# Full-size transposes and last-key products in an attention and MLP kernel on one core

## The chip, the core and the metric

The kernel runs on one core of a Trainium2 chip. The core has five engines that run beside each other and wait for each other by semaphores: TensorE (matrix products; the profile calls it PE, its weight loads PEld), VectorE (DVE), ScalarE (ACT), GpSimd (POOL) and SyncE (SP), which issues most of the DMAs. The metric is the time of one execution on the device in microseconds; of several runs the median counts.

A matrix product on TensorE loads one operand into the array (the weights: so many rows of the array, so many columns) and streams the other through it. In the profile "128\*32 128x128" is a product with 128 rows and 32 columns of the array in use, over a moving operand of 128 rows and 128 columns.

## The reference

Four batches pass through three stages: attention with a decay, a mixing stage of two Fourier transforms with an MLP, and a gated MLP.

```python
scores = scale * np.matmul(q, k.transpose(0, 1, 3, 2))      # 4 x 8 heads, 576 tokens, 64 wide
cum = np.cumsum(np.log(np.clip(f, 0.0001, 1.0)), axis=-1)
scores = np.where(causal, -1e9, scores + cum[:, :, :, None] - cum[:, :, None, :])
scores = scores - np.max(scores, axis=-1, keepdims=True)
attn = np.exp(scores)
attn = attn / (np.sum(attn, axis=-1, keepdims=True) + 1e-09)
x = np.matmul(attn, v)                                       # heads side by side: 4 x 576 x 512
...
u = x + np.real(np.fft.fft(np.fft.fft(x, axis=1), axis=2))
un = (u - mu) / np.sqrt(var + 1e-06)
x = u + np.maximum(un @ w_ch1, 0.0) @ w_ch2                  # 512 -> 2048 -> 512
...
h = np.maximum(x @ w_in, 0.0)                                # 512 -> 1024, halves u and v
v_s = np.einsum('ts,bsd->btd', w_spatial, v_n) + b_spatial[None, :, None]
out = (u * v_s) @ w_out
```

## The kernel before

Each float32 operand is split into two float16 parts, high and low, and a product is made of three float16 products. A batch is handled in steps: the four pairs of heads one after the other (attention), then the folded Fourier transforms, the norm, the MLP of the mixing stage (lines 1052 and 1077: `ph` is the first product, `acc` the second) and the gated MLP (`pu`, `pvv`, `vs`, `po`). While the MLPs of one batch run, the attention of the next is woven in between. TensorE executes in the order in which the code issues: a long written list of steps (`START`) for batch 0 and the attention of batch 1, then tables of times. For the last batches the order on the other engines is set by a scheduler from its own estimates.

For a pair of heads the steps are these. `attn_stack` transposes q and k and sends them by DMA into the tiles `S` (S1 and S2 in the code, two of each in turn). `attn_max` makes the scores once, coarsely, and takes the row maxima with DVE into `mcol`, for five tiles of queries (`QSTART`, `QWIDE`: 128, 128, 64, 128 and 128 queries) and two heads. Its last part, `rows`, writes the negated maxima in two float16 parts into columns 30 and 31 of `mc`, a tile of 128 partitions with 32 columns for each head and query tile, zero elsewhere. Ten transposes (line 692, `mxt`) turn these into rows 96 to 127 of a PSUM tile, and ACT (line 697) and DVE (line 699, one column) copy them into `S`. So the second product of the scores (lines 729 and 733, `sc`) subtracts the maximum as it goes. `mcol` and `mc` exist once and serve all pairs.

`attn_scores` turns the scores into exponentials in `P`, keys down the partitions, in four groups. The 576 keys are four tiles of 128 and one of 64; the group with the last 64 has all 128 partitions of `P` written, those beyond the keys as the exponential of a large negative number. `attn_pv` (lines 797 to 799) multiplies with `vh`, the split v with a column of ones behind each head, of which the sum of the exponentials comes out: `P` is loaded into the array, 65 columns of `vh` are streamed. For the last key tile (`kt == 4`) 64 rows of both were used. `v_prep` allocates `vh` and sets the ones on POOL (line 495), and `v_split` fills it.

Of the first pair of batch 2 the program issues no transposes, so there are 15 groups of ten.

Of the kernel before, what the change touches and what calls it, by code (L numbers as in the profile page):

```python
# [13 lines left out]
F16 = mybir.dt.float16  # L14
# [42 lines left out]
QWIDE = [128, 128, 64, 128, 128]  # L57
# [123 lines left out]
def tile_kernel(  # L181
# [25 lines left out]
    V, A, G, T = nc.vector, nc.scalar, nc.gpsimd, nc.tensor  # L207

    cp = ctx.enter_context(tc.tile_pool(name="cp", bufs=1))
# [20 lines left out]
    o = 0  # L230
# [6 lines left out]
    for h in range(2):  # L237
        CT.append(tab[:, h, 0:963].rearrange("p (t s) -> p t s", t=3))
        ST.append(tab[:, h, 963:1926].rearrange("p (t s) -> p t s", t=3))
        o = 1926  # L240
# [8 lines left out]
    eyeh = cp.tile([128, 128], F16, name="eyeh")  # L249
# [33 lines left out]
    GT = cp.tile([128, 2, 4, 128], F16, name="GT")  # L283
    gsc = cp.tile([128, 1], F32, name="gsc")
    mcol = cp.tile([128, 2, 5], F32, name="mcol")
    mc = cp.tile([128, 2, 5, 32], F16, name="mc")
    G.memset(mc, 0.0)


    state = {}  # L290
# [5 lines left out]
    def xps(name):  # L296
        return pools["x"].tile([128, 2, 512], F32, name=name, tag="x")
# [51 lines left out]
    def smc(b, i):  # L349
        c = 8 * (b % 2) + i  # L350
        return sm[:, c:c + 1]
# [140 lines left out]

    def v_prep(b, raw):
        vh = rp.tile([128, 2, 5, H, 65], F16, name=f"vh{b}", tag="r10")
        G.memset(vh[:, 0, :, :, 64:65], 1.0)
        state[b]["vh"] = vh
        yield
        mx = rp.tile([128, 2], F32, name="vmx", tag="vmx")
        V.memset(mx, 0.0)
        V.tensor_reduce(  # L500
            out=mx[:, 0:1], in_=raw[:, 0:4, :], axis=AX.XY, op=ALU.max, apply_absolute_value=True
        )
        V.tensor_reduce(
            out=mx[:64, 1:2], in_=raw[:64, 4, :], axis=AX.X, op=ALU.max, apply_absolute_value=True
        )
        V.tensor_tensor(mx[:, 0:1], mx[:, 0:1], mx[:, 1:2], op=ALU.max)
        yield 1
        yield from pow2_scale(mx[:, 0:1], smc(b, 0), smc(b, 1), VT)
        V.tensor_scalar(
            out=smc(b, 2), in0=smc(b, 0), scalar1=smc(b, 0), scalar2=1e-6, op0=ALU.mult, op1=ALU.mult  # L510
        )
        yield
# [79 lines left out]
    def attn_max(b, hp):  # L592
        s = hp % 2

        def mm(ps, j, c0, t, k0, k1, mask=None):
            pe_mask = mask is not None and b in PEMASK
            T.matmul(
                ps[:, j, c0:c0 + k1 - k0],
                S2[s][0:126, j, QSTART[t]:QSTART[t] + 128],
                S2[s][0:126, j, QN + k0:QN + k1],  # L600
                start=True, stop=not pe_mask,
            )
            if pe_mask:
                c1 = c0 + k1 - k0
                T.matmul(ps[:, j, c1 - mask.shape[1]:c1], eyeb, mask, start=False, stop=True)

        junk = mo = None

        def work():
            nonlocal junk, mo  # L610
            if mo is None:
                junk = rp.tile([128, 128], BF16, name="junk", tag="junk")
                mo = rp.tile([128, 2], F32, name="mo", tag="mo", bufs=2)

        def diag(ps, t, c0, n, mask, first):
            for j in range(2):
                V.tensor_tensor_reduce(
                    out=junk[:, 0:n], in0=ps[:, j, c0:c0 + n], in1=mask, scale=1.0,
                    scalar=-3.0e38 if first else mo[:, j:j + 1],
                    op0=ALU.add, op1=ALU.max, accum_out=mcol[:, j, t:t + 1],  # L620
                )

        def off(ps, c0, n, dst=None):
            V.tensor_reduce(out=mo if dst is None else dst, in_=ps[:, :, c0:c0 + n], axis=AX.X, op=ALU.max)  # L624

        def both(ps, t, c0, n, mask):

            m = mask.shape[1]
            if b in PEMASK:
                off(ps, c0, n, mcol[:, :, t])  # L630
            else:
                if n > m:
                    off(ps, c0, n - m)
                diag(ps, t, c0 + n - m, m, mask, n == m)

        def diags():
            work()
            pd = xps("mxd")
            for j in range(2):
                mm(pd, j, 0, 0, 0, 128, n0)  # L640
                mm(pd, j, 128, 1, 0, 256, n0)
            yield 1
            both(pd, 0, 0, 128, n0)
            both(pd, 1, 128, 256, n0)
            yield 1

        def wide():
            work()
            pa = xps("mxa")
            for j in range(2):  # L650
                mm(pa, j, 0, 4, 0, 448)
            yield 1
            off(pa, 0, 448)
            yield 1

        def ends():
            pb = xps("mxb")
            for j in range(2):
                mm(pb, j, 0, 4, 448, 576, n4)
                mm(pb, j, 128, 2, 0, 320, n2)  # L660
            yield 1
            if b in PEMASK:
                off(pb, 0, 128, mcol[:, :, 4])
                V.tensor_tensor(mcol[:, :, 4], mcol[:, :, 4], mo, op=ALU.max)
            else:
                diag(pb, 4, 0, 128, n4, False)
            both(pb, 2, 128, 320, n2)
            yield 1

        def rest():  # L670
            work()
            p3 = xps("mxc")
            for j in range(2):
                mm(p3, j, 0, 3, 0, 448, n3)
            yield 1
            both(p3, 3, 0, 448, n3)
            yield

        def rows():
            V.tensor_tensor(  # L680
                mc[:, :, :, 30], mcol, neg.unsqueeze(2).broadcast_to([128, 2, 5]), op=ALU.mult
            )
            V.scalar_tensor_tensor(
                out=mc[:, :, :, 31], in0=mcol, scalar=-1.0 / 16384.0, in1=mc[:, :, :, 30],
                op0=ALU.mult, op1=ALU.subtract,
            )
            yield 1
            pm = pools["x"].tile([128, 2, 1024], F16, name="mxt", tag="x")
            for j in range(2):
                for t, o in enumerate(QSTART):  # L690
                    n = QWIDE[t]
                    T.matmul(  # L692
                        pm[96:128, j, o:o + n], mc[:n, j, t, :], eyeh[:n, :n],
                        is_transpose=True, start=True, stop=True,
                    )
            yield 1
            A.activation(out=S2[s][96:128, :, 0:S], in_=pm[96:128, :, 0:S], func=AF.Copy)
            yield
            V.tensor_copy(S2[s][96:128, :, S:S + 1], pm[96:128, :, 288:289])
            yield 1  # L700

        return dict(d=diags(), a=wide(), b=ends(), c=rest(), t=rows())


# [80 lines left out]
    def attn_pv(b, hp, P):  # L785
        vh = state[b]["vh"]
        ps = xps("pv")
        for g in range(4):
            for j in range(2):
                h = 2 * hp + j  # L790
                for t, c0, n, kt in ((t, *x[1:]) for t in range(5) for x in PV[t] if x[0] == g):
                    kk = 64 if kt == 4 else 128
                    o0 = 65 * t
                    hi = P[g][:kk, 0, j, c0:c0 + n]
                    lo = P[g][:kk, 1, j, c0:c0 + n]
                    first, last = (g, t) == (0, 0), g == 3 and (t, kt) == PVLAST
                    T.matmul(ps[:n, j, o0:o0 + 65], hi, vh[:kk, 0, kt, h, :], start=first, stop=False)  # L797
                    T.matmul(ps[:n, j, o0:o0 + 64], hi, vh[:kk, 1, kt, h, 0:64], start=False, stop=False)  # L798
                    T.matmul(ps[:n, j, o0:o0 + 65], lo, vh[:kk, 0, kt, h, :], start=False, stop=last)  # L799
            yield  # L800
        yield 1

        if "X" not in state[b]:
            state[b]["X"] = yp.tile([128, 5, DM], F32, name=f"X{b}", tag="X")
        X = state[b]["X"]
        rc = rp.tile([128, 2, 5], F32, name="rc", tag="rc")
        po = ps[:, :, 0:325].rearrange("p j (t d) -> p j t d", d=65)
        V.tensor_scalar(out=rc, in0=po[:, :, :, 64], scalar1=16.0e-9, scalar2=None, op0=ALU.add)
        V.reciprocal(rc, rc)
        V.tensor_tensor(  # L810
            X[:, :, 2 * D * hp:2 * D * hp + 2 * D].rearrange("p t (j d) -> p j t d", j=2),
            po[:, :, :, 0:64], rc.unsqueeze(3).broadcast_to([128, 2, 5, 64]), op=ALU.mult,
        )
        yield 1
# [466 lines left out]
    def xsteps(b, small=False):  # L1281
# [5 lines left out]
        def vload():  # L1287
            raw[b] = v_load(b)
            yield 1
            yield from v_prep(b, raw[b])  # L1290
# [160 lines left out]
```

## Time and profile before

| | before |
|---|---|
| median of 3 runs | 928.03 us (924.24 to 930.45) |
| the profiled execution | 930.1 us, its span 928.3 us |
| TensorE busy, weight loads busy | 834.6 us, 721.4 us |
| DVE, ACT, POOL busy | 570.9, 383.2, 196.5 us |
| mean granted clock of TensorE | 0.967 |

The span runs from the first to the last instruction in the trace; the execution's own time has a little around it. Busy times of TensorE overlap, since products are pipelined: the distance between two starts says what a product costs in a full queue, its duration how long it is under way. A row of the chain of waits says what the end of the program depended on at that time.

### The profile page before, as it was taken

The page shows a single profiled execution, that of the slowest core. Times are in us where ns is not written, and L with a number is a line of the kernel's source. Part 1 is how long each engine was busy: PE and PEld are TensorE (multiplying, and loading weights), DVE is VectorE, ACT ScalarE, POOL GpSimd, SP SyncE. Part 2 cuts the span into 40 slices and gives each one's busy share as a digit, 9 for nine tenths or more (in the row PEclk, how much of TensorE's full clock was granted, in tenths as well). Part 3 has the DMA queues.
Part 4 walks back from the last instruction along what each step waited for, and adds up shares of the span by engine and source line. Part 5 has one row for each costly group of instructions (what it writes and reads, how often), then busy time and mean ns, then how long its engine had stood idle before and what let it go on. Part 6 is the DMA issues. An engine that isn't in the chain of part 4 may idle for free.

```text
span 928.3 us, 22154 instructions
## 1 busy us (share of the span) xinstructions
PE 834.6 (90%) x9395; PEld 721.4 (78%) x9395; DVE 570.9 (61%) x1311; ACT 383.2 (41%) x653; POOL 196.5 (21%) x307
## 2 busy tenths in 40 slices
PE   2668359999998998999999998999999999999997
PEld 1456248999997686899997775899997787999784
DVE  5676789897646895746747664747656671123341
ACT  2676656765534433433432442533342432111232
POOL 5276764112013320000005330000004340000010
PEclk9988778999998999999999999999999999999999
DMA  9986157664210008230100017221100001000001
GB/s 184 215 244 224 46 161 178 156 146 122 52 32 5 1 8 180 66 65 2 41 1 2 1 27 172 65 44 23 40 2 1 1 1 47 1 1 2 1 2 57
DMA packets 74835, 60.88 MB, mean 66 GB/s; under 512 B 59680, under 2 KB 60080, under 8 KB 74608
## 3 DMA queue, kind: packets, MB, share of 16 engines
q1 hardware_dynamic: 74016, 58.13, 25.4%
q8 instruction: 74, 1.21, 0.6%
q0 software_dynamic: 720, 1.33, 0.5%
q14 instruction: 25, 0.20, 0.1%
HBM read 40.43 MB, written 4.83 MB: 49 GB/s over the span
## 4 chain that ended last, share of the span: by engine, by line
PE 66%; DVE 13%; ACT 9%; DMA 5%; issue 3%; SPq 2%; POOL 1%; ACTq 0%; DVEq 0%; POOLq 0%
PE ph L1052 17%; PE acc L1077 16%; PE vs L1224 5%; PE pu L1158 5%; PE po L1254 4%; PE pvv L1178 3%; DMA S<-a 2%; ACT P L753 2%; PE pv L797 2%; PE pv L799 1%; PE mxt L692 1%; PE sc L729 1%; PE pv L798 1%; PE yps L914 1%; PE sc L733 1%
## 5 line engine op out<-in xcount | busy, mean ns | idle before, releaser
L1052 PE MATMUL ph<-unT,W 128*128 128x192 f16 x2304 | 208.5, 248 | 1.7 <-DVE unT L1019 1.0
L1077 PE MATMUL acc<-hT,W 128*128 128x192 f16 x2304 | 205.1, 246 | 0.0
L1052 PEld LDWEIGHTS <-W 128*128 128x128 f16 x2304 | 193.6, 99 | 6.9 <-issue 2.6
L1077 PEld LDWEIGHTS <-W 128*128 128x128 f16 x2304 | 191.1, 98 | 0.6
L1059 ACT ACTIVATE hT<-ph 128x384 f16<-128x384 f32 x96 | 47.2, 492 | 146.3 <-PE ph L1052 146.1
L1061 DVE SCALAR_TENSOR_TENSOR hT<-ph,hT 128x384 f16<-128x384 f32 x96 | 53.1, 553 | 86.7 <-ACT hT L1059 86.6
L753 ACT ACTIVATE P<-sc,log 128x642 f16<-128x642 f32 (+3 forms) x64 | 59.2, 933 | 63.7 <-DVE sc L746 53.1
L768 DVE TENSOR_TENSOR P<-sc,P 128x1024 f16<-128x1024 f32 (+3 forms) x50 | 49.6, 994 | 38.4 <-ACT sc L766 36.8
L797 PE MATMUL pv<-vh,P 128*128 128x65 f16 (+1 forms) x480 | 59.9, 204 | 3.7 <-DVE mcol L624 2.4
L729 PE MATMUL sc<-S 128*128 128x256 f16 (+2 forms) x288 | 51.9, 242 | 11.0 <-ACT ex L762 4.9
L799 PE MATMUL pv<-vh,P 128*128 128x65 f16 (+1 forms) x480 | 59.0, 201 | 2.0 <-POOL P L764 1.5
L798 PE MATMUL pv<-vh,P 128*128 128x64 f16 (+1 forms) x480 | 59.1, 201 | 0.0
L1224 PE MATMUL vs<-WP,vn 128*128 128x288 f16 x448 | 57.0, 286 | 0.0
L1178 PE MATMUL pvv<-WI,unT 128*128 128x512 f16 (+1 forms) x240 | 55.7, 388 | 0.3 <-ACT vr L1191 0.3
L733 PE MATMUL sc<-S 128*128 128x256 f16 (+2 forms) x288 | 53.1, 242 | 0.0
L1158 PE MATMUL pu<-unT,WI 128*128 128x192 f16 x576 | 52.0, 250 | 0.8 <-ACT gu L1167 0.8
L797 PEld LDWEIGHTS <-P 128*128 128x128 f16 (+1 forms) x480 | 47.8, 104 | 5.5 <-issue 1.8
L1224 PEld LDWEIGHTS <-vn 128*128 128x128 f16 x448 | 43.6, 98 | 10.7
L1158 PEld LDWEIGHTS <-WI 128*128 128x128 f16 x576 | 48.9, 100 | 3.1 <-issue 2.3
L798 PEld LDWEIGHTS <-P 128*128 128x128 f16 (+1 forms) x480 | 48.3, 105 | 2.8 <-issue 2.6
L799 PEld LDWEIGHTS <-P 128*128 128x128 f16 (+1 forms) x480 | 48.4, 105 | 2.6 <-POOL P L764 1.8
L565 POOL COPY a<-a 128x2 f16<-128x2 f16 x32 | 7.1, 229 | 196.4 <-ACT a L557 177.0
(233 smaller groups left out, 1474.6 us busy)
## 6 DMA issues: line engine op xcount, KB each, us to landing
S<-a SPq DMA_DIRECT2D x96, 144.2 KB, 3.9
W<-in_moe_w_ch_dram SPq DMA_DIRECT2D x16, 512.0 KB, 6.6
WI<-in_moe_w_ch_dram SPq DMA_DIRECT2D x16, 512.0 KB, 5.2
a<-in_k_dram SPq DMA_DIRECT2D x32, 144.0 KB, 3.1
a<-in_q_dram SPq DMA_DIRECT2D x32, 144.0 KB, 4.7
vraw<-in_v_dram SPq DMA_DIRECT2D x16, 256.0 KB, 5.1
WP<-in_moe_w_in_dram SPq DMA_DIRECT2D x8, 512.0 KB
out_dram<-ob SPq DMA_DIRECT2D x16, 256.0 KB, 3.0
```

What stands on the lines that cost most here:

```text
L729: T.matmul(ps[:, j, c0:c0 + w], S2[s][:, j, QN + 128 * kt:QN + 128 + 128 * kt], qh, start=i == 0, stop=False,)
L733: T.matmul(ps[:, j, c0:c0 + w], S1[s][:, j, 128 * kt:128 * kt + 128], q1, start=False, stop=last and b not in PEMASK,)
L753: A.activation(out=pt[:, 0], in_=src, func=AF.Exp, scale=1.0 / 2048.0, bias=log16)
L797: T.matmul(ps[:n, j, o0:o0 + 65], hi, vh[:kk, 0, kt, h, :], start=first, stop=False)
L798: T.matmul(ps[:n, j, o0:o0 + 64], hi, vh[:kk, 1, kt, h, 0:64], start=False, stop=False)
L799: T.matmul(ps[:n, j, o0:o0 + 65], lo, vh[:kk, 0, kt, h, :], start=False, stop=last)
L1052: T.matmul(ph[:, c, :], W1[:, a, kc, 128 * ff:128 * ff + 128], unT[:, e, kc, tok(t)], start=(c == 0 and kc == 0 and i == 0), stop=(c == 1 ...
L1061: V.scalar_tensor_tensor(out=hT[:, 1], in0=ph, scalar=0.0, in1=hT[:, 0], op0=ALU.max, op1=ALU.subtract)
L1077: T.matmul(acc[t][d // 2][:, d % 2, :], W2[:, a, ff, 128 * d:128 * d + 128], hT[:, e, c, :], start=(ff == 0 and i == 0 and d % 2 == 0), st ...
L1158: T.matmul(ph[:, c, :], WI[:, a, kc, 128 * ff:128 * ff + 128], xT[:, e, kc, tok], start=(c == 0 and kc == 0 and i == 0), stop=(c == 1 and ...
L1178: T.matmul(pv[:n, :], xT[:, a, kc, 128 * i:128 * i + n], WI[:, e, kc, DM:2 * DM], start=(kc == 0 and j == 0), stop=(kc == 3 and j == 2),)
L1224: T.matmul(ps, vn[:kk, a, s, 128 * c:128 * c + 128], WP[:kk, e, s, tok], start=i == 0, stop=i == len(jobs) - 1,)
```

## The change

The ten transposes of a pair now use all 128 rows and columns: the tile `mc` gets 96 zero columns in front, so that the 128 columns that end with a block can be loaded, and the block still comes out on rows 96 to 127. The 64-wide piece of the third query tile becomes 128 wide; the next piece overwrites what it writes too much. The products over the last 64 keys use 128 rows; for that, the rows 64 to 127 of `vh` in the last key tile are cleared by a memset on POOL before the ones are set.

```diff
-    mc = cp.tile([128, 2, 5, 32], F16, name="mc")
-    G.memset(mc, 0.0)
+    mcw = cp.tile([128, 416], F16, name="mc")
+    mc = mcw[:, 96:].rearrange("p (j t c) -> p j t c", j=2, t=5)
+    G.memset(mcw, 0.0)
...
         vh = rp.tile([128, 2, 5, H, 65], F16, name=f"vh{b}", tag="r10")
+        G.memset(vh[64:128, :, 4], 0.0)
         G.memset(vh[:, 0, :, :, 64:65], 1.0)
...
                 for t, o in enumerate(QSTART):
-                    n = QWIDE[t]
                     T.matmul(
-                        pm[96:128, j, o:o + n], mc[:n, j, t, :], eyeh[:n, :n],
+                        pm[:, j, o:o + 128], mcw[:, 160 * j + 32 * t:160 * j + 32 * t + 128], eyeh,
                         is_transpose=True, start=True, stop=True,
                     )
...
-                    kk = 64 if kt == 4 else 128
                     o0 = 65 * t
-                    hi = P[g][:kk, 0, j, c0:c0 + n]
-                    lo = P[g][:kk, 1, j, c0:c0 + n]
+                    hi = P[g][:, 0, j, c0:c0 + n]
+                    lo = P[g][:, 1, j, c0:c0 + n]
                     first, last = (g, t) == (0, 0), g == 3 and (t, kt) == PVLAST
-                    T.matmul(ps[:n, j, o0:o0 + 65], hi, vh[:kk, 0, kt, h, :], start=first, stop=False)
-                    T.matmul(ps[:n, j, o0:o0 + 64], hi, vh[:kk, 1, kt, h, 0:64], start=False, stop=False)
-                    T.matmul(ps[:n, j, o0:o0 + 65], lo, vh[:kk, 0, kt, h, :], start=False, stop=last)
+                    T.matmul(ps[:n, j, o0:o0 + 65], hi, vh[:, 0, kt, h, :], start=first, stop=False)
+                    T.matmul(ps[:n, j, o0:o0 + 64], hi, vh[:, 1, kt, h, 0:64], start=False, stop=False)
+                    T.matmul(ps[:n, j, o0:o0 + 65], lo, vh[:, 0, kt, h, :], start=False, stop=last)
```

On TensorE no instruction changes its place. On POOL the memset is added in each batch. Between batches 2 and 3, behind the last norms of the batch before (`st`), POOL's order was:

```order
L994 TENSOR_TENSOR st_7684<-st_7684,mhalf 128x1 x3
L994 TENSOR_TENSOR st_7684<-st_7684,mhalf 65x1
L495 MEMSET vh_8168 128x40
L565 COPY a_7447<-a_7447 128x2 x6
L1145 COPY tsc<-sc_8093 128x2
```

The changed kernel has there, with line numbers two or so higher:

```order
L994 TENSOR_TENSOR st_7687<-st_7687,mhalf 128x1 x3
L994 TENSOR_TENSOR st_7687<-st_7687,mhalf 65x1
L496 MEMSET vh_8171 64x2x520
L497 MEMSET vh_8171 128x40
L567 COPY a_7450<-a_7450 128x2 x6
L1145 COPY tsc<-sc_8096 128x2
```

The new memset stands ahead of the old one, and the copies into `a` (the stacks' last columns) behind both. On DVE the scheduler moved one instruction, in the first pair of batch 3, where the scale of v (`sm`) is worked out from its maximum (`p2e`). Before:

```order
L338 TENSOR_SCALAR sm<-p2e 128x1
L342 TENSOR_SCALAR sm<-p2e 128x1
L699 COPY S_0_93<-mxt 32x2
L509 TENSOR_SCALAR sm<-sm 128x1
L522 SCALAR_TENSOR_TENSOR vh_8168<-vraw_8018,sm,vh_8168 128x8x64 x4
```

And now:

```order
L339 TENSOR_SCALAR sm<-p2e 128x1
L343 TENSOR_SCALAR sm<-p2e 128x1
L511 TENSOR_SCALAR sm<-sm 128x1
L700 COPY S_0_93<-mxt 32x2
L524 SCALAR_TENSOR_TENSOR vh_8171<-vraw_8021,sm,vh_8171 128x8x64 x4
```

The copy that completes `S` with the maxima stands one place later, behind the last step of the scale.

## Rows read from the trace of the kernel before

**Rows 1.** The page, TensorE's busy tenths in 40 slices of the span.
```profile
PE   2668359999998998999999998999999999999997
```

**Rows 2.** The page, chain that ended last, by engine and by line.
```profile
PE 66%; DVE 13%; ACT 9%; DMA 5%; issue 3%; SPq 2%; POOL 1%; ACTq 0%; DVEq 0%; POOLq 0%
PE ph L1052 17%; PE acc L1077 16%; PE vs L1224 5%; PE pu L1158 5%; PE po L1254 4%; PE pvv L1178 3%; DMA S<-a 2%; ACT P L753 2%; PE pv L797 2%; PE pv L799 1%; PE mxt L692 1%; PE sc L729 1%; PE pv L798 1%; PE yps L914 1%; PE sc L733 1%
```

**Rows 3.** Line 692: form, count, min/median/max ns, first and last start.
```profile
L692 PE MATMUL mxt<-eyeh,mc x150: 199/219/314, 35.4 to 681.0; 128*32 128x128 f16 x120, 64*32 64x64 f16 x30
```

**Rows 4.** Timeline of TensorE, batch 3: start us, duration us, engine, line.
```profile
678.94 0.19 PE L797 MATMUL pv<-vh,P 128*65 128x65 f16 x1
678.97 0.20 PE L798 MATMUL pv<-vh,P 128*65 128x64 f16 x1
679.01 0.20 PE L799 MATMUL pv<-vh,P 128*65 128x65 f16 x1
679.13 0.22 PE L797 MATMUL pv<-vh,P 64*65 64x65 f16 x1
...
679.35 0.20 PE L797 MATMUL pv<-vh,P 128*128 128x65 f16 x1
679.39 0.19 PE L798 MATMUL pv<-vh,P 128*128 128x64 f16 x1
...
680.02 0.19 PE L799 MATMUL pv<-vh,P 128*128 128x65 f16 x1
680.14 1.09 PE L692 MATMUL mxt<-eyeh,mc 128*32 128x128 f16 x10
681.16 2.15 PE L1052 MATMUL ph<-unT,W 128*128 128x192 f16 x24
```

**Rows 5.** Timeline of TensorE at 78 us, masks with 128 moving columns.
```profile
78.28 0.22 PE L605 MATMUL mxd<-cmt 128*128 128x128 bf16 x1
78.33 0.27 PE L597 MATMUL mxd<-S 126*128 126x256 f16 x1
```

**Rows 6.** Chain in order of time, 545 to 552 us: start us, us, what.
```profile
547.15 0.88 PE tr L1007 x8
548.03 3.44 PE vs L1224 x28
```

**Rows 7.** Groups of instructions by form: busy us, mean ns, idle before.
```profile
L739 PEld LDWEIGHTS <-cmt 128*128 128x128 bf16 x80 | 7.9, 99 | 1.0
...
L692 PEld LDWEIGHTS <-mc 128*32 128x32 f16 x120 | 7.0, 97 | 4.2 <-issue 2.2
L797 PE MATMUL pv<-vh,P 64*65 64x65 f16 x32 | 7.0, 219 | 0.0
```

**Rows 8.** POOL's groups by form.
```profile
L276 POOL MEMSET S<- 32x1156 f16 x2 | 2.1, 1058 | 0.1
```

**Rows 9.** Timeline of POOL, between batches 2 and 3.
```profile
551.59 0.29 POOL L495 MEMSET vh<- 128x40 f16 x1 [10.53 <-PE vs L1224]
562.82 0.19 POOL L565 COPY a<-a 128x2 f16<-128x2 f16 x1 [10.95 <-ACT a L557]
```

**Rows 10.** Timeline of DVE, first pair of batch 3.
```profile
586.34 0.17 DVE L699 COPY S<-mxt 32x2 f16<-32x2 f16 x1
586.54 0.21 DVE L509 TENSOR_SCALAR sm<-sm 128x1 f32<-128x1 f32 x1
```

**Rows 11.** Chain in order of time, 55 to 212 us.
```profile
55.61 1.03 PE mxt L692 x10
...
73.20 1.48 PE mxt L692 x10
...
211.24 6.55 DMA WP<-in_moe_w_out_dram
```

**Rows 12.** Busy time by stretches: PE, PEld, DVE, ACT, POOL, clock, DMA, GB/s.
```profile
574.47:577.38 2.91, 2.91 (x26) 2.80 (x25) 2.07 (x6) 0.00 (x0) 0.00 (x0) 0.69 0.75 227
577.76:579.74 1.98, 1.98 (x25) 1.92 (x24) 1.74 (x6) 0.14 (x1) 0.00 (x0) 1.00 0.00 0
```

## The prediction

> **What bounds the kernel now.** I read the page first, then the chain of work that ended last, then single matmuls in the timeline. In 40 slices of the span TensorE is busy for 8 tenths and more from the seventh slice on, the last one excepted [rows 1]. The busy share says little by itself, since matmuls overlap; the chain says more: 66% of the span lies on TensorE, mostly in the products of the channel MLP (ph, acc), with 1% in the groups that this change rewrites first (mxt) and 4% in the three lines of pv [rows 2]. So in most of the run a nanosecond taken from TensorE's queue is a nanosecond off the end. The exception is the first sixth of the span: there TensorE is half idle, and the chain runs over DMAs, ACT and DVE.
>
> The durations of matmuls (about 200 ns each) are latencies. What one costs in a full queue is the distance between two starts, and that is what I count.
>
> **The transposes of the maxima.** There are 150 of them, 15 groups of ten: 120 with 128 rows and 30 with 64, all on 32 columns of the array [rows 3]. A group of the last batch shows the price [rows 4]: the last pv product starts at 680.02, the first transpose only at 680.14, the first product behind the group at 681.16. So 0.12 us to get in, and 1.02 us for ten. What would they cost at full size? The nearest row is a product with 128 rows, 128 columns, 128 moving columns and a fresh weight load each time, the masks at 78.28 us: the next starts 0.05 to 0.06 us later [rows 5]. Ten of these are 0.56 us, and the way in is a normal step of about 0.03 us. Before 1.14, after 0.59: 0.55 us less for a group. The two 64-wide pieces grow to 128 columns; this is in the 0.56 already.
>
> Why does a group cost twice its streaming time? Either the transpose itself is slow or the change between array shapes is. The transposes of the spectral stage have full width, and eight of them take 0.88 us, 0.11 us each for 128 float32 columns, with the gate products right behind, 28 in 3.44 us, 0.123 us each, and no gap between [rows 6]. So transposing costs nothing extra, and the shape does. In a group the shape changes six times (in, to 64 rows and back for each of two heads, out), and 0.55 us over six is 0.09 us for one change.
>
> The price from both sides: the least is nothing gained, if full transposes had to wait for their larger weight load (a rival below); the most is 0.55 us plus what rounding hides, 0.02 us. I take 0.55, since the row at 78.28 has the shape that the new ones have. A loss is excluded by the same row as long as loads are hidden.
>
> The rule against this change stands in the Trainium skill, TensorE: Matmul & The Clock Gate, section "LDWEIGHTS (loading the stationary operand)": a weight load takes its number of columns divided by 1.2, so 128 columns would need 107 ns where 32 need 27. By it ten transposes would take 1.07 us, and the groups would gain only their way in. The trace has 97 ns for a load of 32 columns and 99 ns for one of 128 [rows 7], which does not bear the rule out as a limit.
>
> **The products over the last 64 keys.** Three for each head, in 32 blocks, two in a pass of pv [rows 7]. They have 64 rows in the array, their neighbours 128. The last product before the block starts at 679.01, the first of the block at 679.13, the first behind it at 679.35: 0.34 us for four steps [rows 4]. Products with the same 65 columns and 128 rows have starts 0.035 us apart (678.94 to 679.01, two steps, same rows). Four of them are 0.14 us. So 0.20 us less for a block, 0.40 us for a pass, 16 passes. The moving side stays 65 wide, so the extra rows cost no time. Bounds: nothing (if the switch had another reason than rows) and 0.21.
>
> **What is added.** POOL gets a memset of vh, 64 partitions by 2x520 halfwords, four times, ahead of the one that is there. A memset of 1156 halfwords takes 1.06 us (2.1 us for two) [rows 8], so this one is about 0.95 us. In the last batch the old memset runs at 551.59, and POOL's next instruction, the copy into a, starts at 562.82, having waited 10.95 us for ACT [rows 9]. The order shown with the change has these copies right behind the memset. 0.95 us in a hole of 11 us is nothing; without that hole it would delay the copies, the transfers into S and the first maxima of the batch by 0.95 us, at most four times. The first products of pv, which read vh, come tens of microseconds later. The memset of mc grows from 320 to 416 halfwords at the start of the program, some 0.1 us on POOL ahead of the clearing of S; I cost it at 0, at most 0.1.
>
> **What is moved.** On DVE one pair changes places in the last batch: the copy that completes S now stands behind a multiplication of one column. That multiplication takes 0.20 us from start to start [rows 10], and the copy is on the chain there, since the next transposes of q take the PSUM buffer that it frees. So 0.2 us is given back, once.
>
> **What of it lies on the path.** Of the 15 groups, 12 stand in the chain as a block of ten: the ones at 55.61 and 73.20 in batch 0 [rows 11], three in batch 1, three in batch 2 (its first pair has none) and four in batch 3. 12 times 1.02 us is 12.2 us, which is 1.3% of the span and agrees with the 1% of the chain. Missing are the first and the fourth of batch 0, where the chain runs over ACT and POOL, and the second of batch 1, behind which a DMA of 6.55 us for the weights is the last to arrive [rows 11]. Of the 16 passes 11 stand in the chain with their 64-row blocks: one in batch 0, two in batch 1, all eight of batches 2 and 3. The group at 73.20 takes 1.48 us, half as long again as the others; what slows it will slow full-size transposes as well, so I give it 0.5 and not more.
>
> Sum: 11 x 0.55 + 0.5 = 6.55 for the transposes, 11 x 0.40 = 4.4 for the blocks, 0.2 lost on DVE: 10.75 us. The profiled execution took 930.1 us, so 919.3; it was 2.1 us above the median of the runs, 928.03, and so I forecast a median of **917.3 us**, 1.2% less. The runs of before spread from 924.24 to 930.45; a median of such runs may lie some 3 us to either side, 914 to 920.
>
> **Rivals.**
> First, *the early gain is swallowed*. Before 350 us DMAs, ACT and DVE own long pieces of the chain; what TensorE saves there may be waited away. Left are batches 2 and 3: 7 x 0.55 + 8 x 0.40 - 0.2 = 6.85 us, 921.2 us. For it: the DMA at 211 us [rows 11]. Against it: those DMAs are themselves started by the work ahead of them and move up with it.
> Second, *everything counts*: waits that the chain puts down to others are moved up too. 15 x 0.55 + 32 x 0.20 - 0.2 = 14.45 us, 913.6 us.
> Third, *the weight load shows*: a group of full transposes costs ten times the 99 ns of a load [rows 7], 0.99 us, and only 1.14 - 0.03 - 0.99 = 0.12 us is gained. 12 x 0.12 + 4.4 - 0.2 = 5.6 us, 922.4 us. Against it: the pv product at 679.35 has a full load, and the next starts 0.04 us later [rows 4]. The Trainium skill's rule on weight loads (TensorE: Matmul & The Clock Gate, cited above) is the one by which it would come out so.
> Fourth, *it does not do what it says*: the extra 0.09 us belongs to the operands (mc, the 64 keys) and not to the shape. Then the time stays at 928. Against it: going in and coming out cost alike, whoever the neighbour is.
> Fifth, *slower, by the clock*. TensorE reaches the products behind each group earlier, while ACT's copy of the maxima and DVE take as long as before; if it then stands still and its clock falls, 24 products of ph can cost 2.91 instead of 1.98 us, as at 574 us, behind a wait for a DMA, where the granted clock was 0.69 on average (part of the stretch at 1.2 GHz, the rest at 2.4) against 1.00 at 578 us [rows 12]. That is 0.93 us a time, and from 12 such falls on (one behind each group on the path) the gain of 10.75 is gone; with one behind each of the 15 groups the kernel takes 931 us. Against it: behind a group MLP products of 2 us are queued that wait for nobody [rows 4].
>
> **How the numbers follow.** The forecast has a chance of 0.62, the early gain swallowed 0.16, everything counts 0.09, the weight load 0.07, no effect 0.03, slower 0.03. The range that holds 8 in 10 runs from 911 (everything counts, and a low reading) to 923 us (the weight load shows). One per cent, about what a measurement of this kernel can tell from no change, is 918.7 us. The forecast lies 1.4 us below it, so I give it three in four of falling below; with the second rival and a little of the first that makes 0.58 for faster, 0.39 for the same, 0.03 for slower.
>
> **What would show it.** In the timeline of the changed kernel the ten transposes should stand as one form, 128*128, starting 0.055 us apart, with a whole group in 0.56 us; the steps round the 64-key block should be 0.035 us like their neighbours. POOL's copies after the memset should start at the same distance from ACT's release. Rows of TensorE waiting for S or for P that grow by half a microsecond would show gains being waited away. A group that still takes 1 us, or TensorE's clock at half behind the groups, would prove me wrong.

## The result, and the profile after

| | before | after |
|---|---|---|
| median (4 runs each) | 926.13 us (924.2 to 930.45) | 914.89 us (913.98 to 918.21) |
| profiled execution, its span | 930.1 us, 928.3 us | 918.21 us, 916.3 us |
| ratio, 95% interval | | 0.9879, 0.9832 to 0.9926 |

The change made the kernel 1.2% faster; the forecast was 917.3 us in a range of 911 to 923. A second measurement, in more runs (6 and 11), gave 915.35 against 926.41 us, a ratio of 0.9885 (0.9862 to 0.9908), which is 10.65 us less (8.5 to 12.8). The ratios are of the means of the runs, and what is given below as "us less" is worked out from them, so it differs a little from the difference of the medians. The sum had said 10.75.

The page of the changed kernel, TensorE's busy time and the chain by engine and line, the counterpart of [rows 2]:

```profile
PE 818.9 (89%) x9395; PEld 715.3 (78%) x9395; DVE 572.1 (62%) x1311; ACT 383.1 (42%) x653; POOL 201.3 (22%) x311
...
PE 65%; DVE 13%; ACT 9%; DMA 6%; SPq 3%; issue 3%; POOL 2%; ACTq 0%; DVEq 0%; POOLq 0%
PE ph L1052 17%; PE acc L1077 16%; PE vs L1224 5%; PE pu L1158 5%; PE po L1254 4%; PE pvv L1178 3%; DMA S<-a 3%; ACT P L754 2%; PE sc L730 1%; PE yps L914 1%; PE sc L734 1%; PE pv L797 1%; PE pv L799 1%; PE pv L798 1%; ACT sc L767 1%
```

TensorE executes as many products as before (9395) in 15.7 us less busy time, and `mxt` has left the list of the chain. The engines' shares moved by a point at most, and only `ACT sc` (line 767, 1%) has come in at the list's end.

The timeline of TensorE in batch 3, the same pass and the same group as [rows 4] (start us, duration us, engine, line):

```profile
670.25 0.20 PE L799 MATMUL pv<-vh,P 128*65 128x65 f16 x1
670.28 0.20 PE L797 MATMUL pv<-vh,P 128*128 128x65 f16 x1
...
670.73 0.19 PE L799 MATMUL pv<-vh,P 128*128 128x65 f16 x1
670.76 0.72 PE L693 MATMUL mxt<-eyeh,mc 128*128 128x128 f16 x10
671.31 1.90 PE L1052 MATMUL ph<-unT,W 128*128 128x192 f16 x21
```

From the last product of pv to the first transpose 0.03 us pass, and from there to the first product behind the group 0.55 us: 0.58 where [rows 4] had 1.14.

The same kernel's groups by form, the counterpart of [rows 3, 7]:

```profile
L693 PE MATMUL mxt<-eyeh,mc 128*128 128x128 f16 x150 | 11.8, 231 | 2.3 <-DVE mo L626 1.2 <-DVE mc L685 1.1
L693 PEld LDWEIGHTS <-mc 128*128 128x128 f16 x150 | 9.9, 104 | 2.8 <-issue 1.6 <-DVE mc L685 1.2
```

All 150 transposes have one form. Their loads have four times the columns and last 104 ns where they lasted 97, and the products still start 55 ns apart: a load runs under the products ahead of it.

POOL between batches 2 and 3, as in [rows 9]:

```profile
545.40 0.96 POOL L496 MEMSET vh<- 64x1040 f16 x1 [10.53 <-PE vs L1224]
...
556.63 0.18 POOL L567 COPY a<-a 128x2 f16<-128x2 f16 x1 [9.93 <-ACT a L559]
```

The new memset takes 0.96 us, and the wait for ACT behind the two memsets is 9.93 us where it was 10.95: the memset lies in the hole, and the copy comes when ACT releases it.

### The profile page after: what moved, and what is told of

Same layout as the page of the kernel before. It is cut to its first block, busy times and chain, and to the rows that moved or that the text cites. A ratio compares the mean times of both kernels' runs of the same rounds, so it can differ in the third digit from the quotient of the medians.

```text
span 916.3 us, 22159 instructions
## 1 busy us (share of the span) xinstructions
PE 818.9 (89%) x9395; PEld 715.3 (78%) x9395; DVE 572.1 (62%) x1311; ACT 383.1 (42%) x653; POOL 201.3 (22%) x311
## 4 chain that ended last, share of the span: by engine, by line
PE 65%; DVE 13%; ACT 9%; DMA 6%; SPq 3%; issue 3%; POOL 2%; ACTq 0%; DVEq 0%; POOLq 0%
PE ph L1052 17%; PE acc L1077 16%; PE vs L1224 5%; PE pu L1158 5%; PE po L1254 4%; PE pvv L1178 3%; DMA S<-a 3%; ACT P L754 2%; PE sc L730 1%; PE yps L914 1%; PE sc L734 1%; PE pv L797 1%; PE pv L799 1%; PE pv L798 1%; ACT sc L767 1%
## 5 line engine op out<-in xcount | busy, mean ns | idle before, releaser
L797 PE MATMUL pv<-vh,P 128*128 128x65 f16 (+1 forms) x480 | 52.1, 200 | 4.1 <-DVE mcol L626 2.4
L799 PE MATMUL pv<-vh,P 128*128 128x65 f16 (+1 forms) x480 | 51.8, 200 | 2.4 <-POOL P L765 2.1
L798 PE MATMUL pv<-vh,P 128*128 128x64 f16 (+1 forms) x480 | 52.0, 199 | 0.0
L797 PEld LDWEIGHTS <-P 128*128 128x128 f16 (+1 forms) x480 | 46.8, 104 | 3.2 <-issue 1.8
L799 PEld LDWEIGHTS <-P 128*128 128x128 f16 (+1 forms) x480 | 46.6, 104 | 3.1 <-POOL P L765 2.7
L798 PEld LDWEIGHTS <-P 128*128 128x128 f16 (+1 forms) x480 | 46.8, 104 | 2.8 <-issue 2.6
```

Source lines behind the costliest of these rows:

```text
L797: T.matmul(ps[:n, j, o0:o0 + 65], hi, vh[:, 0, kt, h, :], start=first, stop=False)
L798: T.matmul(ps[:n, j, o0:o0 + 64], hi, vh[:, 1, kt, h, 0:64], start=False, stop=False)
L799: T.matmul(ps[:n, j, o0:o0 + 65], lo, vh[:, 0, kt, h, :], start=False, stop=last)
```

## The experiments

Two measures are used. One is the median against the kernel before, which scatters by some 2 us. The other is a ruler in the trace, which does not: from the first `ph` product behind the first pair of batch 2 to the first `acc` product behind the last pass of that batch. TensorE is busy there for 117.97 of 120.03 us before and for 114.53 of 116.58 after, at a granted clock of 1.00 throughout, so its waits (2.06 and 2.05 us) don't move. The stretch holds three groups of transposes and four passes (eight 64-key blocks). Its two ends, before and after:

```profile
375.44 0.50 PE L1052 MATMUL ph<-unT,W 128*128 128x192 f16 x4
...
495.47 0.49 PE L1077 MATMUL acc<-hT,W 128*128 128x192 f16 x4
```

```profile
372.70 0.49 PE L1052 MATMUL ph<-unT,W 128*128 128x192 f16 x4
...
489.28 0.49 PE L1077 MATMUL acc<-hT,W 128*128 128x192 f16 x4
```

That is 120.03 and 116.58 us; two more profiles of these kernels gave 120.02 and 116.57. The table has the ruler of every kernel. "Changes" counts how many changes of the array's shape the edit takes out of the stretch (or puts in): six for a group, two for a block.

| kernel | start, end, us | length | less than before | changes out | us for one |
|---|---|---|---|---|---|
| before | 375.44, 495.47 | 120.03 | | | |
| after | 372.70, 489.28 | 116.58 | 3.45 | 18 + 16 | 0.101 |
| transposes alone | 368.19, 486.52 | 118.33 | 1.70 | 18 | 0.094 |
| last keys alone | 373.14, 491.41 | 118.27 | 1.76 | 16 | 0.110 |
| memsets alone | 373.00, 493.03 | 120.03 | 0.00 | 0 | |
| rows of the transposes alone | 369.83, 488.78 | 118.95 | 1.08 | 12 | 0.090 |
| blocks of a pass together | 373.97, 493.11 | 119.14 | 0.89 | 8 | 0.111 |
| products in turn | 377.33, 500.86 | 123.53 | -3.50 | -32 | 0.109 |
| batches 2 and 3 alone | 372.88, 489.45 | 116.57 | 3.46 | 34 | 0.102 |
| batches 0 and 1 alone | 371.78, 491.79 | 120.01 | 0.02 | 0 | |
| after, with a wider value tile (below) | 366.72, 483.30 | 116.58 | 3.45 | 34 | 0.101 |

The same stretch in batch 3 gives the same differences to within 0.05 us. The rows with the transposes hide a little of the price: two pieces of each group grew from 64 to 128 moving columns, which by the steps of full-size products (0.03 us with 65 moving columns, 0.056 with 128) is some 0.05 us more for a group. With that added back the 0.094 and the 0.090 are both 0.10, and all rows lie between 0.10 and 0.11 us for one change.

**The two parts apart.** First the transposes alone:

```diff
-                        pm[96:128, j, o:o + n], mc[:n, j, t, :], eyeh[:n, :n],
+                        pm[:, j, o:o + 128], mcw[:, 160 * j + 32 * t:160 * j + 32 * t + 128], eyeh,
```

> Only the transposes at full size (with the wider mc), the products over the last 64 keys as before, no memset of vh. If each change of array shape costs 0.09 us of TensorE's queue, a group of ten takes 0.59 instead of 1.14 us, and of 15 groups 12 lie on the path: 6.6 us less than before, minus 0.1 to 0.2 for the copy moved on DVE, so 6.4 us (0.7%). If everything counts, 15 x 0.55 = 8.2 us. If the weight load of 128 columns shows, 1.5 us and transposes 0.099 us apart in the timeline instead of 0.056.

Measured: 917.5 against 927.18 us, 0.9901 (0.9881 to 0.992), so 9.2 us less (7.4 to 11.0). Then the last keys alone, with their memset:

```diff
+        G.memset(vh[64:128, :, 4], 0.0)
...
-                    kk = 64 if kt == 4 else 128
+                    kk = 128
```

> Only the products over the last 64 keys with 128 rows, with the memset of vh, transposes as before. By the shape: 0.20 us less for each of 32 blocks, 22 of them on the path: 4.4 us less than before (0.5%); the steps round the block 0.035 us like their neighbours. By the rival that the products over the last keys cost by themselves (their operands), the steps into and out of the block stay at 0.12 us and the time does not move.

Measured: 920.92 us, 0.9936 (0.9915 to 0.9958), so 5.9 us less (3.9 to 7.9). In the ruler the parts add up, 1.70 and 1.76 us against 3.45 at once, which is 0.57 us for a group and 0.22 for a block. In the whole time they don't: 15.1 us apart, 10.65 together, a gap that is only a little wider than the three intervals allow. That is taken up below.

**The memsets alone**, with nothing on TensorE changed:

```diff
-    mc = cp.tile([128, 2, 5, 32], F16, name="mc")
-    G.memset(mc, 0.0)
+    mcw = cp.tile([128, 416], F16, name="mc")
+    mc = mcw[:, 96:].rearrange("p (j t c) -> p j t c", j=2, t=5)
+    G.memset(mcw, 0.0)
...
+        G.memset(vh[64:128, :, 4], 0.0)
```

> Only what the change adds on POOL: the memset of vh (0.96 us, four times) and the wider memset of mc; TensorE's work as before. If these are hidden in POOL's holes of 8 to 11 us, the time is that of before within its scatter, and the copies into a behind the memset start at the same distance from the release by ACT. If they are not, up to 4 x 0.95 us more (0.4%).

Measured: 926.65 us, 0.9992 (0.9965 to 1.0018). What POOL got costs nothing that can be measured (the interval reaches from 3.2 us less to 1.7 more).

**Is it the shape?** If the change of shape is what costs, the kernel before must get slower when it changes oftener, with the same products on the same operands. The three 64-row products of the last query tile were issued in turn with three 128-row products of that tile:

```diff
+                prods = [(*x, i) for x in jobs for i in range(3)]
+                if g == 3:
+                    mixed = [x for x in prods if x[0] == 4]
+                    mixed.sort(key=lambda x: (x[4], x[3] != 4))
+                    prods = [x for x in prods if x[0] != 4] + mixed
```

> The kernel before, with more shape changes and nothing else: the three 64-row products of a block and the three 128-row products of the same query tile are issued in turn, so that a block has six changes of shape instead of two. The same products on the same operands. If a change costs 0.09 us, 4 x 0.09 = 0.37 us more for a block, 32 blocks, 12 us more on TensorE; on the path 22 blocks, 8.3 us, up to 12 if all counts (0.9 to 1.3% slower), and steps of about 0.12 us all through the block. If the extra belongs to the operands, nothing changes.

Measured: 939.07 us, 1.0152 (1.0113 to 1.019), 14 us more (10.5 to 17.6). Here are the same six products and the step behind them at the end of a head in batch 2, first of the kernel before, then in turn, then of the changed kernel (timelines of TensorE):

```profile
495.03 0.20 PE L799 MATMUL pv<-vh,P 128*65 128x65 f16 x1
495.15 0.22 PE L797 MATMUL pv<-vh,P 64*65 64x65 f16 x1
...
495.37 0.20 PE L797 MATMUL pv<-vh,P 128*128 128x65 f16 x1
...
495.47 0.49 PE L1077 MATMUL acc<-hT,W 128*128 128x192 f16 x4
```

```profile
499.98 0.20 PE L808 MATMUL pv<-vh,P 128*65 128x65 f16 x1
500.10 0.35 PE L804 MATMUL pv<-vh,P 64*65 64x65 f16 x2
...
500.67 0.35 PE L808 MATMUL pv<-vh,P 64*65 64x65 f16 x2
500.86 0.33 PE L1086 MATMUL acc<-hT,W 128*128 128x192 f16 x2
```

```profile
489.06 0.20 PE L799 MATMUL pv<-vh,P 128*65 128x65 f16 x1
489.09 0.20 PE L797 MATMUL pv<-vh,P 128*65 128x65 f16 x1
...
489.28 0.49 PE L1077 MATMUL acc<-hT,W 128*128 128x192 f16 x4
```

From the product ahead (128\*65, all rows) to the first of `acc` it takes 0.44 us with two changes, 0.88 with six, 0.22 with none: 0.11 us for each change, whichever way it goes. A line with x2 holds two products, one of each shape. The durations of single products stay at 0.19 to 0.22 us; the price is only in the distance between starts.

**Fewer changes without larger products.** The two 64-row blocks of a pass stand side by side, with the same rows as before:

```diff
+            jobs = [(j, t, *x[1:]) for j in range(2) for t in range(5) for x in PV[t] if x[0] == g]
+            jobs.sort(key=lambda x: x[4] != 4)
```

> The kernel before, with the two 64-row blocks of a pass (one for each head) moved together to the front of their group: two changes of shape in a pass instead of four, the products the same. If a change of shape costs 0.09 us, 0.19 us less for a pass, 16 passes 3.0 us on TensorE, 2.1 us on the path (0.2%, hardly to be told in time; the timeline shows it: one step of about 0.12 us into the first block, 0.035 between the blocks, one out of the second). If 64-row products cost by themselves, four long steps remain.

Measured: 922.16 against 927.6 us, 0.9946 (0.9927 to 0.9965), 5.0 us less (3.2 to 6.8). A pass has 0.22 us less in the ruler (0.89 over four). In the timeline the way in and the way out remain, and the step from one head to the other costs nothing extra:

```profile
672.59 0.20 PE L801 MATMUL pv<-vh,P 128*128 128x65 f16 x1
672.72 0.22 PE L799 MATMUL pv<-vh,P 64*65 64x65 f16 x1
...
672.84 0.20 PE L799 MATMUL pv<-vh,P 64*65 64x65 f16 x1
...
672.90 0.20 PE L801 MATMUL pv<-vh,P 64*65 64x65 f16 x1
673.03 0.20 PE L799 MATMUL pv<-vh,P 128*128 128x65 f16 x1
```

0.13 us in, 0.13 us out, 0.04 between the heads.

**Rows or columns?** The third tile's transposes got all 128 rows, but still 32 columns, in the kernel before:

```diff
-                        pm[96:128, j, o:o + n], mc[:n, j, t, :], eyeh[:n, :n],
+                        pm[96:128, j, o:o + 128], mc[:, j, t, :], eyeh,
```

> The kernel before, with the transposes of the third query tile on all 128 rows like the others, still on 32 columns of the array. Of six changes of shape in a group four go. If a change costs the same whether rows or columns change, a group takes 1.14 - 4 x 0.09 + 0.06 (two pieces grow from 64 to 128 moving columns), about 0.8 us; steps inside 0.055 to 0.065, the way in 0.12 and the way out 0.15 us as before. If the columns are what costs, a group stays near 1.1 us. The time of one execution does not tell 4 us from nothing.

Measured: 917.34 us in a single run, which says little by itself. The group in batch 3:

```profile
669.27 0.19 PE L798 MATMUL pv<-vh,P 128*128 128x65 f16 x1
669.39 0.73 PE L691 MATMUL mxt<-eyeh,mc 128*32 128x128 f16 x10
670.06 0.26 PE L1051 MATMUL ph<-unT,W 128*128 128x192 f16 x1
```

0.12 us in and 0.67 for the rest, 0.79 together. Before it was 1.14, after 0.58. So without the four changes of rows the group is 0.35 us shorter although two pieces stream 0.05 us more: 0.40 us, 0.10 each. The two that are left, of columns alone, cost 0.21 us, 0.1 each.

**Late and early apart.** The change in batches 2 and 3 alone, then in batches 0 and 1 alone (the memsets in all four both times):

```diff
-                    kk = 64 if kt == 4 else 128
+                    kk = 64 if kt == 4 and not (b >= 2) else 128
```

> Both parts of the change in batches 2 and 3 only; memsets everywhere. If there the queue of TensorE is the path: 7 groups x 0.55 + 16 blocks x 0.21 = 7.2 us, minus 0.1 for the copy moved on DVE, so 7.1 us less than before (0.8%), and in the trace against before a shift that grows by 0.55 us at each group and 0.21 us at each block and never shrinks except where the clock differs.

> Both parts in batches 0 and 1 only; memsets everywhere. By the sum of the prediction: 5 groups on the path (2.7 us) and 3 passes (1.2 us), 3.9 us less than before (0.4%). If the early gain is swallowed by DMAs, ACT and DVE: about nothing. If everything counts: 8 x 0.55 + 16 x 0.21 = 7.8 us. TensorE's steps are those of the changed kernel up to 300 us and those of before after it.

Measured: late 918.87 us, 0.9919 (0.989 to 0.9948), 7.5 us less (4.8 to 10.2); early 925.27 us, 0.9964 (0.9945 to 0.9984), 3.3 us less (1.5 to 5.1). Together 10.8, and the whole change gives 10.65.

**The changed kernel again, and one step further.** The fifth token tile of the gated MLP (`pvv`) has 64 columns of the array where its neighbours have 128. In the kernel tried here it has 128 too; `unT` got 64 cleared columns behind for that:

```diff
-            n = 128 if i < 4 else 64
+            wide = state[b]["unTw"]
...
-                        pv[:n, :], xT[:, a, kc, 128 * i:128 * i + n], WI[:, e, kc, DM:2 * DM],
+                        pv, wide[:, (4 * a + kc) * S + 128 * i:(4 * a + kc) * S + 128 * i + 128],
+                        WI[:, e, kc, DM:2 * DM],
```

> The changed kernel once more, beside before on the same chip, for a narrower interval and beside the next one. By the prediction 10.75 us less than before (ratio 0.9884); by the rival that the early gain is swallowed 0.9926; by the one that everything counts 0.9844.

> The changed kernel, and the last 64 tokens of the value product of the gated MLP (pvv, the fifth tile) with 128 columns of the array instead of 64, the rows beyond the tokens not read; the tile unT gets 64 cleared columns behind it for that, cleared on POOL, and sm is halved to make room. In the trace of before the step into these products takes 0.309 and the step out 0.311 us where 0.216 is normal. If shape is what costs, eight changes of shape go, 8 x 0.094 = 0.75 us, all on the path in batches 1 to 3: 0.6 to 0.75 us less than the changed kernel, too little for the time to tell, visible in the timeline as steps of 0.216 us. By the rival: the steps stay at 0.31.

Measured: 915.35 us (0.9885, as above) and 912.23 us, 0.9863 (0.9839 to 0.9888). The wider tile is the fastest version, but the two intervals overlap. The end of that tile in batch 1, of the changed kernel and of this one (timelines):

```profile
513.83 1.03 PE L1178 MATMUL pvv<-WI,unT 128*64 128x512 f16 x4
514.78 0.42 PE L1158 MATMUL pu<-unT,WI 128*128 128x192 f16 x3
```

```profile
506.06 1.03 PE L1180 MATMUL pvv<-WI,unT 128*128 128x512 f16 x4
506.93 0.49 PE L1160 MATMUL pu<-unT,WI 128*128 128x192 f16 x4
```

The last four products and the step behind them take 0.95 and 0.87 us. So 128 columns cost no more than 64, and the way out of the narrower shape costs about 0.09 us here too, with 512 moving columns. Eight such changes (in and out, four batches) are 0.7 us; the medians differ by 3.1 us, and the shape does not explain the rest. What can be seen is that this kernel's profile has no stretch at a fallen clock between 300 and 900 us, and each of the two profiles of the changed kernel has three.

**The kernel before again**, for its clock and its start:

> The kernel before once more, unchanged, for its trace alone. If the stretches of TensorE in batches 2 and 3 are its own work and nothing else, the way from the first ph behind the first pair to the first acc behind the last pv takes 120.0 us again, to 0.05 us. If the falls of the granted clock at 508, 573 and 720 us belong to the kernel, they stand at the same places; if they come and go with the run, some are missing, and each missing one moves all that follows by 1.5 to 2 us.

Measured: 927.09 us in a single run, the ruler 372.25 to 492.27, 120.02 us. The half-clock stretches at 508, 573 and 720 us of the first profile came again, at 505, 570 and 717.

## Why the prediction was right

The prices of the prediction hold, and so does their cause. What it read of the path holds for batches 2 and 3 and only in part for batches 0 and 1, so that the total of 10.75 against 10.65 us is closer than the working behind it.

**The transposes.** Predicted 1.14 to 0.59 us for a group, measured 1.14 to 0.58 in the timeline and 0.57 less in the ruler. The row of the masks [rows 5] had given the right step: 55 ns with fresh 128-column loads.

**The cause.** The prediction blamed the change of shape and got 0.09 us for one from a division, which left out that two of the ten pieces streamed half as many columns before; with these 0.05 us it is 0.10. The cause is shown now from both sides: taking changes out gains 0.10 to 0.11 us each, with transposes or with products, and putting changes in, with the same operands, costs 0.109 each. The rival that the operands were slow is out, since the same products in turn cost twice as much. A change of rows alone costs, and a change of columns alone does too. The Trainium skill, TensorEngine Tiling (Array Packing), section "Key Properties", says that changing the tiling mode drains TensorE. A price at each change, as measured here, fits that; that the engine drains is not shown by it.

The trace shows where the time goes: into the start of the next weight load. Here are the loads of the first transposes in batch 3, before and after (timelines of TensorE's loads):

```profile
680.14 0.11 PEld L692 LDWEIGHTS <-mc 128*32 128x32 f16 x2
```

```profile
670.73 0.13 PEld L693 LDWEIGHTS <-mc 128*128 128x128 f16 x2
```

The last product of pv ahead of them started at 680.02 and at 670.73 us. So the load of the same shape starts with the product ahead of it, and that of another shape 0.12 us behind it, together with its own product (680.14). Nearly all other places are alike. In the trace of the kernel before, from 300 to 900 us, 6374 products follow another of the same shape without a gap (65 and more rows or columns taken as 128), and in all but 106 of these steps the load starts within 5 ns of the start of the product ahead. In the 81 steps with a change of shape it starts 120 to 308 ns behind that, and at most 5 ns ahead of its own product: 0.12 us with 65 moving columns in the product ahead, 0.15 with 128, 0.31 with 512, each time some 0.09 us more than the normal step.

**The last keys.** Predicted 0.20 us for a block, measured 0.22 in the ruler and from 0.44 to 0.22 in the timeline. The 128-row products start 0.03 us apart, no further than the 64-row ones did.

**The size of the weight load** did not show: products with 128-column loads start 55 ns apart. The rule in the Trainium skill (TensorE: Matmul & The Clock Gate, "LDWEIGHTS (loading the stationary operand)") gives a load of 128 columns 107 ns. The loads of the changed kernel last 104 ns on average, but those of 32 columns lasted 97 ns too, and loads overlap each other, so the rule does not bound the distance between products here.

**POOL** costs nothing that shows, as predicted (0.9992, and the hole of 10.53 + 9.93 us round the memsets).

**DVE's swap** was put at 0.2 us. DVE and TensorE in the first pair of batch 3 after the change, the place of [rows 10]:

```profile
579.28 0.21 DVE L511 TENSOR_SCALAR sm<-sm 128x1 f32<-128x1 f32 x1
579.52 0.17 DVE L700 COPY S<-mxt 32x2 f16<-32x2 f16 x1
```

```profile
578.96 0.49 PE L553 MATMUL pk<-cft,a 96*128 96x96 f32 x4
579.75 0.72 PE L553 MATMUL pq<-cft,a 96*128 96x96 f32 x6 [0.30 <-DVE S L700]
```

The copy comes 0.24 us behind the multiplication, and the transposes of q wait 0.30 us for it, where before they did not wait. From the last four transposes of k to the first of q it is 0.79 us now and was 0.61 (585.96 to 586.57), so 0.18 us is lost, once.

**The path.** That 12 of 15 groups and 11 of 16 passes count was read from the chain, and here the agreement is better than the reading deserves. With the measured sizes the sum would be 11 x 0.57 + 0.5 + 22 x 0.22 - 0.2 = 11.4 us, and 15.4 if everything counted; measured are 10.65 (8.5 to 12.8). So the rival by which everything counts is out for the whole change, and the one by which all of the early gain is swallowed is out too, since the early half alone gives 3.3 us (1.5 to 5.1). In batches 2 and 3 the measured 7.5 us (4.8 to 10.2) agree with all on the path: 7 x 0.57 + 16 x 0.22 - 0.2 = 7.3 us. In batches 0 and 1 it is some 40%: 8 x 0.57 + 16 x 0.22 = 8.1 us on TensorE, measured 3.3, where the prediction's sum has 3.9.

Which early groups lie on the chain was read from one profile, and it does not stay. The sum took five of the eight, at 55, 73, 166, 241 and 274 us of the kernel before. A second profile of that kernel has six (33, 53, 71, 201, 239 and 272 us). The two profiles of the changed kernel have four, those near 34, 70, 238 and 270 us, and all seven of batches 2 and 3. The group at 55 us is the clearest: with full-size transposes TensorE now waits ahead of it for DVE's `mc` (1.07 and 1.26 us in the two profiles, none in the two of before), the chain runs over DVE and ACT there, and what TensorE saves at this group no longer shortens it.

The parts by themselves fit this worse. The transposes alone gave 9.2 us (7.4 to 11.0), where the path by the measured sizes allows 11 x 0.57 + 0.5 = 6.8 and everything 8.6. The blocks put side by side gave 5.0 (3.2 to 6.8) against 11 x 0.22 = 2.4 and 16 x 0.22 = 3.5, and the products in turn cost 14 us against 22 x 0.44 = 9.7 and 32 x 0.44 = 14.1. Why each edit alone seems to count nearly in full, and both parts together not, stays open. One candidate can be seen in the changed kernel, at the first wait of batch 2's attention (timeline of TensorE, first before, then after):

```profile
365.40 0.34 PE L597 MATMUL mxd<-S 126*128 126x128 f16 x2 [2.47 <-DMA S<-a]
...
366.21 2.14 PE L1052 MATMUL ph<-unT,W 128*128 128x192 f16 x24
368.19 0.55 PE L597 MATMUL mxb<-S 126*128 126x128 f16 x4
```

```profile
361.09 0.34 PE L599 MATMUL mxd<-S 126*128 126x128 f16 x2 [2.94 <-DMA S<-a]
...
361.96 3.65 PE L1052 MATMUL ph<-unT,W 128*128 128x192 f16 x24
365.45 0.55 PE L599 MATMUL mxb<-S 126*128 126x128 f16 x4
```

TensorE now waits 0.47 us longer for the stacks' DMA, and behind the wait its clock fell: the 24 products take 3.49 us to the next start instead of 1.98. The windows say the same (columns: PE, PEld, DVE, ACT, POOL busy, clock, DMA share, GB/s; the clock was 1.00 in the same place before):

```profile
361.09:365.45 4.36, 4.36 (x30) 3.68 (x31) 2.75 (x10) 0.00 (x0) 0.00 (x0) 0.61 0.41 121
```

This is the step that the rival by which the kernel gets slower counts on (a wait, then a fallen clock), but at one place, behind a DMA and not behind the groups, and for 1.5 us. It stood in both profiles of the changed kernel and in none of the two parts alone. But it is no rule: the wait was 2.94 and 2.84 us in those two, 2.77 in the last keys alone without a fall, and 1.90 and 2.20 in the blocks put together and the products in turn, both with one. More widely, the profiles differ in how many such falls they have between 300 and 900 us: three in both of the kernel before and in both of the changed one, two in the transposes alone, one in the last keys alone and in the blocks put together, four in the products in turn, two and three in the late and the early half alone, none in the rows alone and in the memsets alone. At some 1.5 to 2 us each that is of the size of the gap. As one profile was taken of each part, it is not shown that this is where the parts' surplus comes from.

**The reference run.** The forecast took 2.1 us off because the profiled execution lay above the median. Here the chance of that run can be named: its last transposes of k ahead of the first group started at 28.73 us, those of the second profile of the same kernel at 27.28 and of the changed kernel at 27.03. So of the 11.9 us between the first two profiles 1.7 arise before the first changed product, and the median was the better base. It was still high: in eleven further runs the kernel before took 926.41 us, and the 1.6 us between that and 928.03 are most of the 2.4 by which the forecast of 917.3 lies above the measured 914.89.

## What to carry to other kernels

Count the changes of the array's shape in TensorE's order of work, in rows or in columns, and price each at about 0.1 us: in this kernel small products among full ones were cheaper at full size, with cleared operands, than at their own. Where padding isn't to be had, put the small ones side by side. And price such an edit in the steps of the timeline, and its effect stage by stage: here it counted in full where TensorE is busy throughout (7.5 of 7.3 us), and by some 40% (3.3 of 8.1 us, with a wide interval) in the batches where the chain also runs over DMAs and other engines.

## What the runs showed of the hardware that was not expected

*What counts as a change of shape.* 65 columns beside 128 cost nothing (670.25 to 670.28 us above), and 32 or 64 beside 128 cost some 0.1 us. Of the steps between 65, 66, 96, 126 and 128 rows or columns in the trace of before (300 to 900 us, without a gap), 170 of 173 have the next load start with the product ahead. Nor did 128 transposed columns cost more than 32: ten steps of 55 ns.

*The clock falls in some executions and not in others.* The kernel with the memsets alone has the products of the kernel before, and the ruler to 0.01 us. Yet at the start of batch 2's gated MLP, behind the same wait of 1.93 us for DVE, the clock fell in one and not in the other (timeline of TensorE, kernel before, then memsets alone):

```profile
718.33 0.32 PE L330 MATMUL p2ps<-cft,xmx 128*128 128x128 f32 x1 [1.93 <-DVE xmx L1091]
718.49 2.98 PE L1158 MATMUL pu<-unT,WI 128*128 128x192 f16 x24
721.26 3.63 PE L1178 MATMUL pvv<-WI,unT 128*128 128x512 f16 x12
```

```profile
712.25 0.32 PE L331 MATMUL p2ps<-cft,xmx 128*128 128x128 f32 x1 [1.93 <-DVE xmx L1093]
712.41 2.14 PE L1160 MATMUL pu<-unT,WI 128*128 128x192 f16 x24
714.39 2.75 PE L1180 MATMUL pvv<-WI,unT 128*128 128x512 f16 x12
```

Windows of 16 us round that place, before and memsets alone (the clock is the third number from the end):

```profile
710.00:726.00 16.00, 14.07 (x86) 8.46 (x84) 15.72 (x42) 6.54 (x13) 11.55 (x18) 0.89 0.00 0
```

```profile
710.00:726.00 16.00, 14.07 (x95) 8.53 (x94) 14.12 (x38) 7.76 (x15) 7.20 (x15) 1.00 0.00 1
```

The 24 products take 2.77 us to the next start in the one, part of them at 1.2 GHz, and 1.98 in the other; with the products behind them the fall costs 1.7 us (718.49 to 724.73 against 712.41 to 716.98, 6.24 and 4.57 us). The profile of the memsets alone, at 922.34 us, had no such fall between 300 and 900 us, while both profiles of the kernel before had three there (at 508, 573 and 720 us in the first). So a few falls more or less may well be much of the scatter of some 5 us between runs of one kernel (the runs without a profile can't show it), and a gain of 1% is better read from a stretch in which none lies.
